# Seven block products for two tiles' keys and values, and queries in 512 columns, in a linear-attention and gated-network kernel

## The chip, the cores and the metric

The kernel runs on one core of a Trainium2 chip. The metric is device time in microseconds; the median of three runs of the kernel before is 583.31 us (582.87 to 583.67).

## The reference

All matrix products are fp32. With 2048 tokens of width D = 512, 32 heads of 16 and F = 1376:

```python
xn = layernorm(x)                                  # (2048, 512)
q, k, v = heads(xn @ wqkv)                         # 32 heads of 16
phi(t)  = concat(softmax(t @ w_phi), softmax(-(t @ w_phi)))   # per head, 32 wide
kv, z   = phi(k)^T v, sum_s phi(k)                 # state, over all tokens
s = (phi(q) kv / (phi(q) z + 1e-6)) @ wo
g = silu((relu(xn @ W_gate) * (xn @ W_up)) @ W_down)
out = x + s * g
```

The state needs all keys and values before the first query can be finished.

## The kernel before, in words

**Split products.** Each fp32 product is made of three fp32r matmuls: an operand is kept as a high part (rounded to fp32r by ScalarE) and a low part (the rest, subtracted on VectorE or GpSimd). `mm3` issues low x high, high x low, high x high for each 128 rows of the contraction. A "product" of 256 contraction rows is thus six matmuls.

**Token loop.** Tokens come in 16 tiles of 128, in the order of `order`: tiles of blocks 2 and 3 alternate, then those of blocks 0 and 1 (a block is 512 tokens). Tiles 2m and 2m + 1 make pair m: one tile of each block. Per tile n of the loop `for n in range(N)`: layernorm (sums on ScalarE in `norm_stats`, one power on GpSimd and two tiny operations on VectorE in `norm_scale` and `norm_apply`), transposition on TensorE with two copies on ScalarE (`turn`: `hi_xt`, `full_xt`) and the low part on VectorE (`lo_xt`); keys and values (`project`: 12 matmuls of 512 columns each); `features` (max, min, shift, exponentials, values' high and low parts, sums, reciprocal into PSUM, scaling); `features_split` (high part of phi on ScalarE, low part on GpSimd, and a DMA issued by GpSimd that adds phi to `zacc`); `query` for the tile before (24 matmuls of 256 columns, copied out and stored); `kv_products` of two tiles before (eight matmuls of 256 columns into four PSUM banks that stay until the end of the loop). The key weights are `wk` folded with w_phi on TensorE (`fold`), as are the query weights.

**Gated network.** `gate_up` computes gate and up of one 128-wide slice f (eleven slices) for a pair of blocks with seven products instead of eight (Strassen's scheme in Winograd's form): the transposed inputs `XT` hold blocks A11, A12, A22 and four sums S1 to S4 (`sums_x`, `sums_hi`, `sums_lo`), and `f_prep` makes the weights' differences and their parts (wa, wb, wc, wd) on GpSimd and ScalarE and stores them for the second half. The block A21, not wanted by the seven products, sits in a buffer of its own. Down products follow in chunks of two slices. Queries are finished (`q_pair`, `q_back`) beside this, and `out_tile` ends each half. There are two halves (blocks 0 and 1, then 2 and 3); the inputs of the second are stored and reloaded.

**Order of work.** Instructions of each engine run in the order written. Work in generators (weights' preparation, queries) is put in between by the object `pace`, which counts an estimated clock; constants such as `AHEAD`, `START` and the 20 in `pace.add(all_queries(0), 20)` set when it may begin. `AHEAD = (2, 3)` has slices 2 and 3 prepared in the token loop. `B8, B4, B2` are the numbers of 8, 4 and 2 KB buffers.

The lines of the scaling and the state of PSUM:

```python
        nc.vector.reciprocal(pv[:, 0:64], sm)
        phi = e if n else zacc
        nc.vector.tensor_tensor(groups(phi), groups(e), pv[:, 0:64].unsqueeze(2).to_broadcast([P, 64, DH]), op=ALU.mult)
        ...
            PKV.extend(ps((P, 2, 256), name=s) for s in ("pkv", "pkv", "pkv", "pseed"))
```

Of the kernel before, what the change touches and what calls it, by code (L numbers as in the profile page):

```python
# [13 lines left out]
P = 128  # L14
S = 2048
D = 512
# [12 lines left out]
B8, B4, B2 = 3, 10, 41  # L29
LEAD = 3  # L30
# [118 lines left out]
def layer_kernel(ctx: ExitStack, tc: tile.TileContext, x, wkT, wqT, wv, wo, wf, cst, out):  # L149
# [3 lines left out]
    pp = ctx.enter_context(tc.tile_pool(name="pp", bufs=8, space=bass.MemoryType.PSUM))  # L153
# [56 lines left out]
    N = len(order)  # L210
    X = {}
# [8 lines left out]
    def w_tile(name):  # L220
        return [(u2((P, D), f"{name}h", F32R), u2((P, D), f"{name}l", F32R)) for k in range(KD)]
# [8 lines left out]
    def rows(w):  # L230
        return lambda k: w[k]

    def fold(w, raw, k):

        p = ps(name="pfold")
        for j in range(KD):
            nc.tensor.matmul(p[:, j * P:(j + 1) * P], raw[:, j * P:(j + 1) * P], bd_sb[:, j, :],
                             start=True, stop=True)
        if w is WQ:
            return lambda: split(*w[k], p)  # L240
        return lambda: split(*map(by_parity, w[k]), even_first(p))


    XT = sb.tile([P, 7, 2, 2, BT], F32R, tag="XT", name="XT")
    pace.shared = XT.name
    A21, A21P, XN, XF, SF = {}, {}, {}, {}, {}

    def norm_stats(n):
        xt = X.pop(n)
        xn = u2((P, D), "xn")  # L250
        sm, ss, rs, bias = small(1, "lm"), small(1, "lv"), small(1, "lr"), small(1, "lb")
        nc.scalar.activation(xn, xt, AF.Copy, scale=-1.0 / D, accum_out=sm)
        nc.scalar.activation(xn, xt, AF.Square, bias=sm, accum_out=ss)
        XN[n] = xn, xt, bias, rs, sm, ss

    def norm_scale(n):
        xn, xt, bias, rs, sm, ss = XN[n]
        nc.vector.tensor_scalar(rs, ss, 1.0 / D, 1e-5, op0=ALU.mult, op1=ALU.add)
        nc.gpsimd.tensor_tensor(rs, rs, mhalf, op=ALU.pow)

    def norm_apply(n):
        xn, xt, bias, rs, sm, ss = XN[n]
        nc.vector.tensor_scalar(bias, sm, rs, None, op0=ALU.mult)
        nc.scalar.activation(xn, xt, AF.Identity, bias=bias, scale=rs)
        XN[n] = xn
# [16 lines left out]
    def cols(n):  # L282
        i = order[n][1]
        return slice(i * P, (i + 1) * P)
# [8 lines left out]
    def xt_parts(n, s):  # L293

        if n % 2 == 0:
            return [(XT[:, A11:A12 + 1, s, :, cols(n)], slice(0, 2))]
        if n not in A21:
            if n % 4 == 1:
                A21P[n // 4] = u4((P, 2, 2, 2 * P), "a21", F32R)
            c = n // 2 % 2 * P  # L300
            A21[n] = A21P[n // 4][:, :, :, c:c + P]
        return [(A21[n][:, s], 0), (XT[:, A22, s, :, cols(n)], 1)]

    def hi_xt(n, p):
        for to, c in xt_parts(n, 0):
            nc.scalar.activation(to, p[:, c], AF.Copy)
# [5 lines left out]
    def lo_xt(n, p):  # L312
        for (to, c), (hi, _) in zip(xt_parts(n, 1), xt_parts(n, 0)):
            add(nc.vector, to, p[:, c], f32(hi), ALU.subtract)

    def turn(m, full=True):
        p = transpose_x(m)
        hi_xt(m, p)
        if full:
            full_xt(m, p)  # L320
        return m, p

    def sums_x(n):

        x0, x1 = XF.pop(n - 1), XF.pop(n)
# [5 lines left out]
        SF[n] = sa, sb_  # L331

    def sums_hi(n):
        for s, c in zip(SF[n], (S1, S3)):
            nc.scalar.activation(XT[:, c:c + 2, 0, :, cols(n)], s, AF.Copy)

    def sums_lo(n):
        for s, c in zip(SF.pop(n), (S1, S3)):
            add(nc.gpsimd, XT[:, c:c + 2, 1, :, cols(n)], s, f32(XT[:, c:c + 2, 0, :, cols(n)]), ALU.subtract)

    def xt_cols(n):
        c = cols(n)
        if n % 2 == 0:
            return lambda k: (XT[:, k // 2, 0, k % 2, c], XT[:, k // 2, 1, k % 2, c])
        return lambda k: ((XT[:, A22, 0, k % 2, c], XT[:, A22, 1, k % 2, c]) if k // 2 else
                          (A21[n][:, 0, k % 2, :], A21[n][:, 1, k % 2, :]))

    xt_spill = dram((P, 7, 2, 2, BT), "xts")

    def spill_x(n):  # L350
        nc.sync.dma_start(xt_spill[:, :, :, :, cols(n)].rearrange("p c s k t -> p (c s k) t"),
                          f32(XT[:, :, :, :, cols(n)].rearrange("p c s k t -> p (c s k) t")))


    VH, PHI, PQ, EK = {}, {}, {}, {}
    PKV = []

    def project(n, w, name):
        p = ps(name=name)
        mm3(p, xt_cols(n), rows(w), range(KD))  # L360
        return p

    def query(n):

        b, h, j = order[n - n % 4 + n % 4 // 2][0], n // 4, n % 2
        c = slice(h % 2 * 2 * P, (h % 2 + 1) * 2 * P)

        def x_of(k):
            if n % 4 < 2:
                return XT[:, k // 2, 0, k % 2, c], XT[:, k // 2, 1, k % 2, c]  # L370
            if k // 2:
                return XT[:, A22, 0, k % 2, c], XT[:, A22, 1, k % 2, c]
            return A21P[h][:, 0, k, :], A21P[h][:, 1, k, :]
        p = ps((P, 2, 2 * P), name="pq")
        for d in range(2):
            w = slice((2 * j + d) * P, (2 * j + d + 1) * P)
            mm3(p[:, d, :], lambda k: [t[:, w] for t in WQ[k]], x_of, range(KD))
        if n % 4 == 3:
            A21P.pop(h)
        t = u2((P, 2, 2 * P), "pqs")  # L380
        nc.scalar.activation(t, p, AF.Copy)
        q = 2 * b + h % 2
        PQ[q, j] = dram((P, 2, 2 * P), f"pq{q}{j}")
        pace.when(t, lambda: nc.sync.dma_start(PQ[q, j], t))

    def features(n, pk, pv, between):

        vhl = u4((P, NG, 2, 64), "vhl", F32R)
        pvg = pv.rearrange("p (g f) -> p g f", g=NG)
        pkv_ = pk.rearrange("p (h f) -> p h f", f=DH)  # L390
        sm = small(64, "sm", 2)
        e = u4((P, H, 2, DH), "ek")
        mx = sb.tile([P, 2, H], F32, tag="mx", bufs=2, name="mx")
        nc.vector.tensor_reduce(mx[:, 0, :], pkv_, op=ALU.max, axis=AX.X)
        nc.vector.tensor_reduce(mx[:, 1, :], pkv_, op=ALU.min, axis=AX.X)
        for s in range(2):
            top = mx[:, s, :].unsqueeze(2).to_broadcast([P, H, DH])
            a, b = (top, pkv_) if s else (pkv_, top)
            nc.vector.tensor_tensor(e[:, :, s, :], a, b, op=ALU.subtract)
            nc.scalar.activation(e[:, :, s, :], e[:, :, s, :], AF.Exp)  # L400
            if s == 0:
                nc.scalar.activation(vhl[:, :, 0, :], pvg, AF.Copy)
        between()
        add(nc.vector, vhl[:, :, 1, :], pvg, f32(vhl[:, :, 0, :]), ALU.subtract)
        nc.vector.tensor_reduce(sm, groups(e), op=ALU.add, axis=AX.X)
        nc.vector.reciprocal(pv[:, 0:64], sm)
        VH[n] = vhl
        phi = e if n else zacc
        nc.vector.tensor_tensor(groups(phi), groups(e), pv[:, 0:64].unsqueeze(2).to_broadcast([P, 64, DH]), op=ALU.mult)
        EK[n] = phi  # L410

    def features_split(n):
        phi = EK.pop(n)
        phl = u8((P, NG, 2, P), "phl", F32R)
        split(phl[:, :, 0, :], phl[:, :, 1, :], flat(phi).rearrange("p (g f) -> p g f", g=NG), nc.gpsimd)
        if n:
            nc.gpsimd.dma_start(zacc, phi, accum_op=ALU.add)
        PHI[n] = phl

    def kv_products(n):  # L420
        phl, vhl = PHI.pop(n), VH.pop(n)
        if n == 0:
            PKV.extend(ps((P, 2, 256), name=s) for s in ("pkv", "pkv", "pkv", "pseed"))
# [7 lines left out]
    def two(name, apart):  # L431
        if apart:
            return [u2((P, 2, 2, P), name) for c in range(2)]
        t = u4((P, 2, 2, 2, P), name)
        return [t[:, c] for c in range(2)]
# [3 lines left out]
    def f_load(f):  # L439
        RAW[f] = two("rawg", f not in AHEAD), u2((P, D), "rawd")  # L440
        for c in range(2):
            nc.sync.dma_start(RAW[f][0][c].rearrange("p k s f -> p (k s f)"), wf[f][:, c * 512:(c + 1) * 512])
        nc.sync.dma_start(RAW[f][1], wf[f][:, 1024:])

    def w_pair(name):
        return u2((P, 2, 2, P), name, F32R), u2((P, 2, 2, P), name, F32R)
# [9 lines left out]
    def f_prep(f, keep=True):  # L456


        rg, rd = RAW.pop(f)
        b11, b12, b21, b22 = (rg[c][:, :, s, :] for c in range(2) for s in range(2))  # L460
        ta, tb = two("tab", keep)
        yield "gpsimd", b22
        add(nc.gpsimd, tb[:, 0], b12, b11, ALU.subtract)
        add(nc.gpsimd, ta[:, 1], b22, b12, ALU.subtract)
        wa = w_pair("wa")
        yield "scalar", b11
        for c in range(2):
            nc.scalar.activation(wa[0][:, c], rg[c][:, :, 0, :], AF.Copy)
        put(f, 0, wa[0])
# [4 lines left out]
        yield "scalar", ta  # L474
        nc.scalar.activation(wb[0], ta, AF.Copy)
        put(f, 2, wb[0])
        yield "gpsimd", wa[0]
        for c in range(2):
# [774 lines left out]
```

## Time and profile before

| | |
|---|---|
| median of three runs | 583.31 us |
| the profiled execution | 582.29 us |
| its span, first to last instruction | 580.3 us |
| TensorE busy | 567.5 us |
| GpSimd busy | 407.6 us |
| VectorE busy | 377.9 us |
| ScalarE busy | 297.9 us |
| granted TensorE clock | 1.0 |

In rows of the profile PE is TensorE's matmuls, PEld its weight loads, DVE VectorE, ACT ScalarE, POOL GpSimd. Nearly all rows have line 52, that of the helper through which all instructions are issued, so they are told apart by tile names. Rows of the timeline begin with the start, then the length, both in us; neighbouring instructions of an engine overlap a little, so the spacing of two starts is what one costs in a row of them.

### The profile page before, as it was taken

How to read it: one execution, taken by the hardware profiler on the slowest of the kernel's cores; microseconds unless marked ns; L12 is line 12 of the kernel's file. 1: busy time of each engine (PE TensorE's matmuls, PEld its weight loads, DVE VectorE, ACT ScalarE, POOL GpSimd, SP SyncE). 2: the span in 40 equal slices, each digit the busy share in tenths (PEclk: the TensorE clock that was granted, in tenths of full speed). 3: DMA queues.
4: the chain of work that ended last, by engine and by line, in shares of the span. 5: the costliest groups of instructions: out<-in, count | busy, mean ns of one | idle time of the engine just before them, and what ended most of it. 6: DMA issues, size and time to landing. Idle time of an engine off the chain costs nothing.

```text
span 580.3 us, 8580 instructions
## 1 busy us (share of the span) xinstructions
PE 567.5 (98%) x2848; PEld 478.5 (82%) x2848; DVE 377.9 (65%) x558; ACT 297.9 (51%) x536; POOL 407.6 (70%) x342
## 2 busy tenths in 40 slices
PE   8899999999999999999999999999999999999997
PEld 7788888889898788887888888787888888888786
DVE  3897766768564888998733332589698648943222
ACT  3796876766544547574543243234554634553500
POOL 0779888978868459999977514554568776976393
PEclk9999999999999999999999999999999999999999
DMA  8358899874499928797888999993566775459972
GB/s 299 104 159 222 231 288 291 237 207 99 138 251 283 370 78 274 241 307 255 276 279 281 261 384 406 380 389 127 150 213 201 221 227 188 117 171 311 291 216 108
DMA packets 82523, 138.25 MB, mean 238 GB/s; under 512 B 7600, under 2 KB 30512, under 8 KB 81584
## 3 DMA queue, kind: packets, MB, share of 16 engines
q1 hardware_dynamic: 79024, 125.60, 63.8%
q0 software_dynamic: 3312, 12.06, 11.0%
q8 instruction: 22, 0.36, 0.2%
q14 instruction: 21, 0.17, 0.1%
q10 hardware_dynamic: 144, 0.07, 0.0%
HBM read 77.14 MB, written 52.69 MB: 224 GB/s over the span
## 4 chain that ended last, share of the span: by engine, by line
PE 71%; POOL 9%; DMA 9%; issue 4%; DVE 3%; ACT 2%; SPq 0%; POOLq 0%; ACTq 0%; DVEq 0%
PE py L52 16%; PE pseed L52 12%; PE pd L52 8%; PE pa L52 8%; PE pso L52 8%; PE pq L52 5%; PE pv L52 4%; PE pk L52 4%; DMA wol<-wo 3%; PE pnum L52 2%; DMA pql<-pq 2%; POOL phl L52 2%; POOL XT L52 1%; DMA ws<-wd 1%; PE pkv L52 1%
## 5 line engine op out<-in xcount | busy, mean ns | idle before, releaser
L52 PE MATMUL py<-fdh,hl 128*128 128x512 f32 x176 | 68.8, 391 | 0.6 <-POOL hl L52 0.6
L52 PE MATMUL py<-fdh,hh 128*128 128x512 f32 x176 | 68.5, 389 | 0.0
L52 PE MATMUL py<-fdl,hh 128*128 128x512 f32 x176 | 68.5, 389 | 0.0
L52 POOL TENSOR_TENSOR hl<-e,hh 128x512 fp32r<-128x512 f32 x22 | 29.2, 1328 | 55.8 <-ACT hh L52 54.1
L52 PE MATMUL pa<-XT,wa 128*128 128x512 f32 x264 | 67.6, 391 | 0.0
L52 PE MATMUL pseed<-XT,wb 128*128 128x512 f32 x240 | 62.0, 393 | 1.4 <-ACT u L52 1.0
L52 PEld LDWEIGHTS pa<-XT,wa 128*128 128x128 f32 x264 | 49.2, 188 | 10.4 <-issue 0.5
L52 PEld LDWEIGHTS pseed<-XT,wb 128*128 128x128 f32 x240 | 44.4, 188 | 13.2 <-ACT u L52 3.3
L52 POOL TENSOR_TENSOR phl<-ek,phl 128x1024 fp32r<-128x1024 f32 x15 | 36.5, 2434 | 24.5 <-ACT phl L52 24.5
L52 DVE TENSOR_TENSOR y<-py,y 128x512 f32<-128x512 f32 x40 | 27.6, 691 | 39.9 <-PE py L52 39.7
L52 POOL TENSOR_TENSOR hl<-u,hh 128x512 fp32r<-128x512 f32 x22 | 29.4, 1335 | 19.0 <-ACT hh L52 17.3
L52 POOL TENSOR_TENSOR ez<-eq,zB 128x1024 f32<-128x1024 f32 x16 | 39.4, 2473 | 1.6 <-ACT eq L52 1.6
L52 PEld LDWEIGHTS py<-fdh,hl 128*128 128x128 f32 x176 | 33.0, 188 | 8.2 <-POOL hl L52 1.4
L52 PEld LDWEIGHTS py<-fdh,hh 128*128 128x128 f32 x176 | 33.0, 188 | 6.9
L52 PEld LDWEIGHTS py<-fdl,hh 128*128 128x128 f32 x176 | 33.1, 188 | 6.8
L52 POOL TENSOR_TENSOR y<-y,ys 128x512 f32<-128x512 f32 x24 | 31.1, 1297 | 9.0 <-ACT ys L52 9.0
L52 PE MATMUL pq<-XT,wqh 128*128 128x256 f32 x192 | 35.4, 282 | 0.0
L52 POOL TENSOR_TENSOR ol<-of,oh 128x1024 fp32r<-128x1024 f32 x8 | 19.4, 2439 | 22.2 <-DMA ol<-eq 11.7
L52 PE MATMUL pv<-wvh,XT 128*128 128x512 f32 x96 | 33.2, 400 | 1.0 <-ACT pqs L52 1.0
L52 PE MATMUL pd<-XT,wc 128*128 128x512 f32 x132 | 33.9, 390 | 0.0
L52 PE MATMUL pd<-XT,wd 128*128 128x512 f32 x132 | 33.6, 389 | 0.0
L52 DVE TENSOR_TENSOR e<-pd,e 128x512 f32<-128x512 f32 x22 | 15.1, 687 | 27.5 <-PE pd L52 19.6
(176 smaller groups left out, 1603.4 us busy)
## 6 DMA issues: line engine op xcount, KB each, us to landing
zacc<-ek POOLq DMA_DIRECT2D x15, 512.0 KB, 5.8
xts<-XT SPq DMA_DIRECT2D x4, 1792.0 KB
XT<-xts SPq DMA_DIRECT2D x7, 1024.0 KB, 14.9
wa<-ws SPq DMA_DIRECT2D x26, 256.0 KB, 3.0
wb<-ws SPq DMA_DIRECT2D x26, 256.0 KB, 5.2
wc<-ws SPq DMA_DIRECT2D x26, 256.0 KB, 4.2
rawg<-wf SPq DMA_DIRECT2D x22, 256.0 KB, 3.7
ws<-wa SPq DMA_DIRECT2D x22, 256.0 KB, 2.3
```

The costliest lines, as they stand in the source:

```text
L52: return self.tc.keep_in_program_order(op(*a, **k))
```

## The change

Pairs 2 to 7 take keys and values together in the seven-product scheme that the gated network has: the 512 x 1024 weight (keys beside values) is cut into blocks B11, B21 (keys) and B12, B22 (values) with differences T1 to T4, and the inputs' sums S1 to S4 are those of the network. Pairs 0 and 1 keep eight products, and the differences are made beside them. For pairs 0 and 1 the sums are made later, beside slices 8 and 9. Tile e = 2m, o = 2m + 1:

```diff
-A11, A12, A22, S1, S2, S3, S4 = range(7)
+A21, A22, A11, A12, S1, S2, S3, S4 = range(8)
-B8, B4, B2 = 3, 10, 41
+B8, B4, B2 = 2, 24, 14
-AHEAD = (2, 3)
-START = (12, 15)
+START = (14, 14)
-    pp = ctx.enter_context(tc.tile_pool(name="pp", bufs=8, space=bass.MemoryType.PSUM))
+    pp = ctx.enter_context(tc.tile_pool(name="pp", bufs=7, space=bass.MemoryType.PSUM))
+    seed = pp.tile([P, BT], F32, tag="seed", bufs=1, name="seed")
     def norm_scale(n):
-        nc.vector.tensor_scalar(rs, ss, 1.0 / D, 1e-5, op0=ALU.mult, op1=ALU.add)
+        nc.gpsimd.tensor_scalar(rs, ss, 1e-5, None, op0=ALU.add)
         nc.gpsimd.tensor_tensor(rs, rs, mhalf, op=ALU.pow)
+        nc.gpsimd.tensor_scalar(bias, sm, rs, D ** 0.5, op0=ALU.mult, op1=ALU.mult)
+    def key_scale(n):
+        e, pk, sm = EK[n]
+        r = sm if pk is None else pk[:, 0:64]
+        nc.vector.reciprocal(r, sm)
+        nc.vector.tensor_tensor(groups(e), groups(e), r.unsqueeze(2).to_broadcast([P, 64, DH]), op=ALU.mult)
+    def query(h, d, ks=range(KD)):
+        mm3(p, lambda k: [t[:, k % 2, w] for t in WQ[k // 2]],
+            lambda k: [XT[:, k // 2:k // 2 + 3:2, s, k % 2, c] for s in range(2)], ks, 0 in ks, KD - 1 in ks)
+    for m in range(2, M):
+        e, o = 2 * m, 2 * m + 1
+        pa = ps(name="pa")
+        product(pa, A11, "B11", m, True)
+        nc.scalar.activation(seed, pa, AF.Copy)
+        key_split(e - 2)()
+        query((m - 1) // 2, d + 1)
+        query_out((m - 1) // 2, d + 1)
+        product(seed, S2, "T2", m)
+        nc.scalar.activation(u, seed, AF.Copy)
+        collect = key_split(o - 2)
+        norm_stats(e + 4); norm_scale(e + 4)
+        product(pa, A12, "B21", m)
+        kv_products(e - 2)
+        key_shift(e, pa)
+        sums_x(m + 1)
+        product(seed, S3, "T3", m)
+        nc.scalar.activation(w, seed, AF.Copy)
+        norm_stats(o + 4); norm_scale(o + 4)
+        product(pd, S1, "T1", m, True)
+        key_exp(e)
+        norm_apply(e + 4); norm_apply(o + 4)
+        add(nc.vector, w, pd, w)
+        value_hi(o, w)
+        value_lo(o)
+        key_total(e)
+        product(seed, A22, "T4", m)
+        product(pd, S4, "B22", m)
+        add(nc.vector, u, pd, u)
+        mx = bounds(seed)
+        kv_products(o - 2)
+        collect()
+        px = turn(e + 4)
+        lo_xt(*px)
+        value_hi(e, u)
+        value_lo(e)
+        key_shift(o, seed, mx)
+        sums_hi(m + 1)
+        sums_lo(m + 1)
+        key_scale(e)
+        query(h, d)
+        query_out(h, d)
+        key_exp(o)
+        px = turn(o + 4)
+        key_total(o)
+        lo_xt(*px)
+        key_scale(o)
-            run(gate_up(f, used, rest))
+            run(gate_up(f, nc.gpsimd if half else nc.vector, used, rest))
-                    queries = pace.add(all_queries(0), 20)
+                    queries = pace.add(all_queries(0), 6)
```

(Two calls on a line and the missing conditions for the first and last pairs are shortenings of this text.) `value_lo` runs on GpSimd, `key_split` is the splitting of phi with its DMA returned as `collect`. Each pair has two queries, now of 12 matmuls of 512 columns. The last argument of `gate_up` shown is the engine of the low half hl of the network's hidden values: VectorE in the first half. The first slice is computed like the others, the separate `gate_up_apart` is gone; the last query, and the first half's last output tile, are issued behind the first product of a half's first slice. Small tiles are sized so that the larger buffers begin at multiples of 512 bytes. A21 is now part of XT, and the state's parts take its place after the loop.

More of the change, by code (lines that the diff above doesn't have):

```diff
@@ L728, in q_pair @@
         yield "vector", pv[1]
-        bounds(1)
-        shift(1)
+        bound(1)
+        shifted(1)
         if q + 1 < NP:
```

710 lines of the change are left out of this document (401 added, 309 removed).

## The prediction

> **What bounds the kernel now.** I read the page's busy times and chain of waits first, then three stretches in the windows view (the first four token tiles, the other twelve, the first half of the gated network), then who TensorE waited for.
>
> ```profile
> span 580.3 us, 8580 instructions
> ...
> PE 567.5 (98%) x2848; PEld 478.5 (82%) x2848; DVE 377.9 (65%) x558; ACT 297.9 (51%) x536; POOL 407.6 (70%) x342
> ...
> PE 71%; POOL 9%; DMA 9%; issue 4%; DVE 3%; ACT 2%; SPq 0%; POOLq 0%; ACTq 0%; DVEq 0%
> ```
> ```profile
> 0.00:54.00 54.00, 49.37 (x296) 44.17 (x297) 39.25 (x75) 38.41 (x78) 31.50 (x37) 1.00 0.62 193
> 54.00:176.00 122.00, 120.82 (x744) 107.37 (x743) 83.41 (x129) 77.77 (x148) 101.17 (x96) 1.00 0.80 220
> 176.00:338.00 162.00, 160.57 (x733) 131.57 (x732) 111.34 (x157) 81.06 (x157) 123.67 (x115) 1.00 0.80 266
> ```
> ```profile
> PE pxT L52 <- DVE lr L52: 2.0, 1, 2.0
> ...
> PE pv L52 <- ACT pqs L52: 1.0, 2, 0.7
> ```
>
> The window columns are PE, PEld, DVE, ACT, POOL. TensorE is the bound in every stage: 120.8 of 122 us in the token loop, and its longest wait anywhere is 2.0 us. The reader should also see that POOL is second in the loop (101 of 122). So a removed matmul is worth its spacing, as long as no other engine takes TensorE's place. The spacing comes from the chain (start, length, count):
>
> ```profile
> 54.25 2.75 PE pk L52 x12
> ...
> 130.69 2.84 PE pq L52 x24
> ...
> 134.47 2.75 PE pk L52 x12
> ...
> 176.05 1.39 PE pa L52 x6
> ...
> 337.93 16.32 PE py L52 x72
> ```
>
> A 512-column matmul takes 2.75/12 = 0.229 us in the projections and 16.32/72 = 0.227 in the down products; a 256-column one 2.84/24 = 0.118. Tile 4's keys start at 54.25, tile 12's at 134.47, the gated network at 176.05: four pairs of tiles take 80.2 us (20.06 each), and the last two pairs, with one more query and one more set of key-value products behind them, 41.6.
>
> **The change part by part.** *Seven products.* A pair has 42 instead of 48 projection matmuls: 6 x 0.229 = 1.37 us for six pairs, 8.2. *Queries.* 12 matmuls of 512 for 24 of 256: 2.84 - 12 x 0.227 = 0.12 us, sixteen times, 1.9. Together 10.1 us of TensorE, 1.61 in each pair of the loop. The Trainium skill ("TensorE: Matmul & The Clock Gate", Back-to-back issue gap) gives N/2.4 + 2.5 ns, so 109 and 216 ns; by it a query saves 0.03 us and all of them 0.5, and the forecast below would be up to 1.4 us higher. The trace's 118 and 227 differ from it, and the sum goes by them.
>
> *What the products add.* Each pair gets three more ScalarE copies (pa into seed, seed into u, seed into w) and two VectorE additions, the low halves of both values go from VectorE to GpSimd, and so do two small operations of each layernorm. PSUM for rotating tiles falls from four to three (seven buffers less the four of the key-value sums). Everything is issued in written order, so what counts is the longest loop through the queues. I find it like this. In pair m GpSimd's order is: low part of phi(e-2), collecting DMA, low part of phi(o-2), norm scale (e+4), four input sums, norm scale (o+4). ScalarE's normalisation of tile o+4 waits for the last of these. Behind it stand, in ScalarE's order: high half of value o, turn(e+4) (two copies), high half of value e, two high parts of the sums, query copy, two exponentials, turn(o+4) (two copies), the next pair's seed copy, the next phi high part; and GpSimd's next low part waits for that one. The prices are starts to starts in stretches without idle time, GpSimd first, then ScalarE:
>
> ```profile
> 62.43 2.43 POOL L52 TENSOR_TENSOR phl<-ek,phl 128x1024 fp32r<-128x1024 f32 x1 [2.79 <-ACT phl L52]
> 64.80 0.84 POOL L52 DMA_DIRECT2D zacc<-ek  x1
> 65.43 1.54 POOL L52 TENSOR_TENSOR XT<-sa,XT 128x512 fp32r<-128x512 f32 x1
> ...
> 67.95 0.77 POOL L52 TENSOR_TENSOR lr<-lr,mhalf 128x1 f32<-128x1 f32 x1
> 68.49 0.93 POOL L52 TENSOR_TENSOR sa<-xf 128x256 f32<-128x256 f32 x1
> 69.19 0.93 POOL L52 TENSOR_TENSOR sb<-xf 128x256 f32<-128x256 f32 x1
> 69.89 0.92 POOL L52 TENSOR_TENSOR sa<-sa,xf 128x256 f32<-128x256 f32 x1
> 70.89 0.74 POOL L52 TENSOR_TENSOR sb<-xf,sa 128x256 f32<-128x256 f32 x1
> 71.59 2.43 POOL L52 TENSOR_TENSOR phl<-ek,phl 128x1024 fp32r<-128x1024 f32 x1
> ```
> ```profile
> 60.26 0.61 ACT L52 ACTIVATE XT<-sa 128x512 fp32r<-128x512 f32 x1
> 60.78 0.62 ACT L52 ACTIVATE XT<-sb 128x512 fp32r<-128x512 f32 x1
> 61.30 1.05 ACT L52 ACTIVATE phl<-ek 128x1024 fp32r<-128x1024 f32 x1
> 62.25 0.80 ACT L52 ACTIVATE xn<-xt,lb,lr 128x512 f32<-128x512 f32 x1
> ...
> 63.97 0.63 ACT L52 ACTIVATE ek<-ek 128x512 f32<-128x512 f32 x1
> 64.49 0.60 ACT L52 ACTIVATE vhl<-pv 128x512 fp32r<-128x512 f32 x1
> 64.96 0.64 ACT L52 ACTIVATE ek<-ek 128x512 f32<-128x512 f32 x1
> ...
> 69.78 0.80 ACT L52 ACTIVATE xn<-xt,lb,lr 128x512 f32<-128x512 f32 x1
> 70.49 0.57 ACT L52 ACTIVATE XT<-pxT 128x512 fp32r<-128x512 f32 x1
> 70.97 0.58 ACT L52 ACTIVATE xf<-pxT 128x512 f32<-128x512 f32 x1
> ```
>
> GpSimd: two low parts at 2.37 (62.43 to 64.80), the DMA 0.63, the four sums 3.10 (68.49 to 71.59): 8.47, and two norm scales. ScalarE: normalise 0.71 (69.78 to 70.49), four copies out of PSUM or of values, queries and seed at 0.47 (64.49 to 64.96), four turn copies at 0.48, four operations at 0.52 (60.26 to 60.78, 63.97 to 64.49), phi 0.95 (61.30 to 62.25): 0.71 + 1.88 + 1.92 + 2.08 + 0.95 = 7.54. The hand-overs between the two engines I put at 0.4 (phi ends at 62.35 on ScalarE and GpSimd starts at 62.43; the rest is the part of a last instruction that the spacing leaves out).
>
> A norm scale is now three dependent GpSimd operations on 128x1, of which only the power was there. Rows near the other two:
>
> ```profile
> L1245 POOL MEMSET const-float32-0.0<- 128x1 f32 x1 | 0.1, 99 | 0.2 <-issue 0.2
> ```
> ```profile
> L52 POOL TENSOR_TENSOR lr<-lr,mhalf x12: 549/798/849, 25.2 to 128.3; 128x1 f32<-128x1 f32 x12
> ...
> L52 DVE TENSOR_SCALAR lb<-lm,lr x12: 206/212/216, 25.8 to 129.1; 128x1 f32<-128x1 f32 x12
> ```
>
> Bounds for one norm scale: 0.54 + 0.1 with the rest hidden, or three times the power's 0.54 and twice the 0.3 us that the third sum lost on its predecessor (1.00 instead of 0.70 to the next start), 2.2. I take 0.9, the power plus two at about VectorE's 0.15 to 0.21, the nearest operation of that kind. The loop is then 8.47 + 1.8 + 7.54 + 0.4 = 18.2 us.
>
> One thing more sits in it: the scaling of keys now reads its reciprocals from SBUF instead of PSUM, so this 1024-element VectorE operation has both inputs in SBUF. Such an operation is there today only as pTl:
>
> ```profile
> 254.29 2.13 DVE L52 TENSOR_TENSOR pTl<-ez,pTh 128x1024 fp32r<-128x1024 f32 x1
> ```
> ```profile
> 255.28 2.28 POOL L52 TENSOR_TENSOR wb<-tab,wb 128x512 fp32r<-128x512 f32 x1
> ```
> ```profile
> L52 DVE TENSOR_TENSOR pTl<-ez,pTh x6: 1215/1240/2129, 220.1 to 287.8; 128x1024 fp32r<-128x1024 f32 x6
> ```
> ```profile
> L52 POOL TENSOR_TENSOR wb<-tab,wb 128x512 fp32r<-128x512 f32 x11 | 17.0, 1542 | 0.0
> ...
> L52 POOL TENSOR_TENSOR tab<-rawg 128x256 f32<-128x256 f32 x22 | 17.8, 878 | 0.9 <-PE py L52 0.9
> ```
>
> The two overlapped, and GpSimd's took 2.28 where its mean is 1.54; bounds 0 and about 1 us for each of the two scalings in a pair. Scaling o comes when GpSimd works on the next low part, inside the loop; scaling e during the low parts of the sums, outside it. I count one: 19.2 us. That is above TensorE's own 20.06 - 1.61 = 18.45, so in these four pairs ScalarE and GpSimd set the pace: 4 x 19.2 = 76.8 instead of 80.2, -3.4. Of VectorE's additions none is on this loop; their cover is its 38 us idle in 122. The last two pairs have no layernorm and no turning, the loop is open there, and TensorE's gain counts in full: 2 x 1.61, -3.2.
>
> *The first four tiles* keep eight products. GpSimd gets four weight differences (4 x 2.37) and the low parts of T1 and T4 (4 x 1.54), about 15.6 us more, and loses two sets of sums; ScalarE gets twelve copies at about 0.5; VectorE four low parts and the statistics of two tiles. All still fit in 54 us by the windows row (39, 38 and 31 busy), but VectorE closely. Bounds: -2 (the 2.0 us wait for lr goes) and +6 (15.6 less GpSimd's idle before it is wanted, and VectorE late). I take +0.5. The loop starts with keys 2 and 3 not yet scaled and one pair of exponentials (1.04) ahead of the first phi: +1.0.
>
> *Weights of the gated network.* f = 2 and 3 are no longer prepared in the loop and f = 0, 1 only in its last pair, with the low parts on VectorE. One f costs GpSimd at most 4 x 0.88 and five low parts of 1.54, 11.2 us. f = 2 is wanted about 20 us into the network; bounds 0 and +5, taken +1.0. The low halves hl of half 0 move to VectorE, 22 operations with both inputs in SBUF; their cover is its 51 and GpSimd's 38 idle us of 162, price 0, if it fails a few us. The seeded first product, the last query and the last output tile put between f = 0's products, the sums fetched at f = 8 and 9, and buffers starting at multiples of 512 bytes: 0, hidden under TensorE; bounds -1 and +1.
>
> Sum: -3.4 - 3.2 + 0.5 + 1.0 + 1.0 = -4.1 us. The profiled execution took 582.29 (span 580.3 and 2.0 around it), so 578.2; the median of the runs is 1.0 above it, 583.31, so 579.2.
>
> **The rivals.** *TensorE keeps the pace.* The small GpSimd operations are nearly free and no scaling collides: 8.47 + 1.28 + 7.54 + 0.4 = 17.7, under 18.45. Then the whole 10.1 is won, and the first stage costs nothing: 573. For it: ScalarE and GpSimd have idle time in the loop today. Against: that idle time is waiting for each other (2.79 us before the low part at 62.43).
>
> *The loop through GpSimd is longer than before: slower.* Norm scale at 1.44 (0.54, two of 0.15 and two gaps of 0.3) and both scalings colliding: 8.47 + 2.88 + 7.54 + 0.4 + 2.0 = 21.3, 4 x 21.3 - 80.2 = +5.0; with -3.2 and +2.5 the time is 587.6. It decides from 20.2 us a pair, 1.0 above my number. For it speaks the row at 254.29; against, that it is the longest of six such operations. The Trainium skill ("SBUF — State Buffer", Who interferes with whom) states that a VectorE instruction with two SBUF inputs and a GpSimd instruction that reads SBUF exclude each other. The 2.28 us row agrees.
>
> *The first stage turns VectorE-bound* and ends 5 us later (its 39.25 us there grow by four low parts of 0.6, half a pTl, and two tiles' statistics to about 45, an estimate, and it starts only when the first tile has landed): 583.3, no change.
>
> **How the numbers follow.** Forecast 0.40, TensorE keeps the pace 0.22, longer loop 0.26, late first stage 0.12. A measurement here tells 0.2% (1.2 us) from nothing. Faster: 0.62. The late first stage mostly ends within 1.2 us: same 0.10, and its rest to slower: 0.28. The range is 571 (TensorE's full gain and its present waits) to 588 (the longer loop); the forecast alone is 576 to 582.
>
> **What would show it.** Right: pairs of about 19 us in the first four of the loop and 17 in the last two; TensorE waiting for ScalarE ahead of the seed products (T2) and ScalarE waiting for GpSimd ahead of xn; queries of 12 matmuls in 2.72 us. Wrong: pairs of 18 us without waits (573), or GpSimd rows of phl well over 2.43 and pairs above 20.2 (slower); a loop that starts well after 55 us; a wait at f = 2 for wa or wb.

## The result and the profile after

The changed kernel takes 607.22 us (median of four runs, 604.49 to 610.54) beside 583.49 (582.87 to 583.81) for the kernel before: a ratio of 1.041 (95% interval 1.036 to 1.046). The profiled execution took 607.11. The first lines of its page:

```profile
span 605.3 us, 8090 instructions
...
PE 565.1 (93%) x2616; PEld 462.3 (76%) x2616; DVE 428.7 (71%) x536; ACT 310.1 (51%) x557; POOL 407.7 (67%) x339
```

VectorE has 51 us more than before, GpSimd as much as before. The windows view, cut at the loop's first product, at pair 6, at the network and at its second half (columns PE, PEld, DVE, ACT, POOL, clock, DMA share, GB/s):

```profile
0.00:61.00 61.00, 51.04 (x260) 41.43 (x261) 44.58 (x69) 35.49 (x67) 33.90 (x34) 0.97 0.51 170
61.00:150.00 89.00, 76.16 (x363) 61.32 (x361) 67.40 (x68) 59.35 (x115) 65.86 (x73) 0.98 0.44 119
150.00:187.60 37.60, 34.60 (x164) 28.33 (x165) 34.78 (x32) 20.82 (x36) 29.57 (x25) 1.00 0.58 152
187.60:393.60 206.00, 197.27 (x885) 160.52 (x884) 148.57 (x198) 102.35 (x190) 137.13 (x118) 0.99 0.89 299
393.60:605.00 211.40, 206.01 (x951) 170.75 (x949) 133.35 (x172) 92.04 (x152) 141.24 (x91) 1.00 0.70 224
```

In the pairs no engine is full: TensorE is busy 76 of 89 us, VectorE 67, GpSimd 66. That is a loop of waits, not a full engine. The first starts on TensorE in the trace mark the stages (us; e1, e5 and e11 are experiments below):

| | before | after | e1 | e5 | e11 |
|---|---|---|---|---|---|
| start to the loop's first product | 54.3 | 61.1 | 59.5 | 59.0 | 61.1 |
| pairs 2 to 5 | 80.2 | 88.8 | 81.4 | 73.8 | 73.9 |
| pairs 6 and 7 | 41.6 | 37.8 | 40.3 | 40.3 | 35.9 |
| half 0 | 195.0 | 205.9 | 202.9 | 201.5 | 203.7 |
| half 1 to the span's end | 209.3 | 211.7 | 211.7 | 211.7 | 211.6 |
| span | 580.3 | 605.3 | 595.8 | 586.3 | 586.2 |
| gaps on TensorE, summed | 19 | 55 | 45 | 36 | 36 |

The last row is worked out from the trace: each distance between two starts, less the number of matmuls times their spacing (0.227, 0.119 and 0.111 us for 512, 256 and 128 columns). Matmul records that are missing count as gaps, a few us in each column, and so does what a lower clock takes: the granted clock is 0.992 on the mean after the change and 1.0 before, 0.8% of 605 us, about 5 us. So the change takes about 10 us of matmuls away, as forecast, and adds some 35 us of gaps. The last query moved from the pairs into half 0 and the last output tile from half 0 into half 1, 12 matmuls or 2.7 us each; a set of eight key-value products (1.0 us) moved from the pairs into half 0 too.

Who waits for whom, TensorE first, then ScalarE (us in total, times, longest):

```profile
PE pkv L51 <- POOL phl L51: 8.8, 5, 2.0
PE seed L51 <- ACT u L51: 8.5, 10, 2.2
PE seed L51 <- ACT seed L51: 4.1, 4, 2.0
PE pa L51 <- DVE XT L51: 3.7, 4, 1.5
```
```profile
ACT phl L51 <- DVE ek L51: 27.6, 14, 3.1
...
ACT xn L51 <- POOL lb L51: 13.2, 6, 2.8
```

The scaling of keys in the groups view, before and after (behind the bar the busy us of all, the mean ns of one, and the idle us before them):

```profile
L52 DVE TENSOR_TENSOR ek<-ek,pv 128x1024 f32<-128x1024 f32 x15 | 18.3, 1220 | 0.5
```
```profile
L51 DVE TENSOR_TENSOR ek<-ek,sm 128x1024 f32<-128x1024 f32 x15 | 41.7, 2777 | 0.5
```

One cycle of a pair in the timeline of the changed kernel, TensorE, VectorE, GpSimd:

```profile
105.38 0.50 PE L51 MATMUL pa<-B11h,XT 128*128 128x512 f32 x1 [1.47 <-DVE XT L51]
...
127.65 0.50 PE L51 MATMUL pa<-B11h,XT 128*128 128x512 f32 x1 [1.42 <-DVE XT L51]
```
```profile
104.63 0.69 DVE L51 TENSOR_TENSOR XT<-pxT,XT 128x512 fp32r<-128x512 f32 x1 [2.84 <-ACT xf L51]
...
106.94 3.84 DVE L51 TENSOR_TENSOR ek<-ek,sm 128x1024 f32<-128x1024 f32 x1
...
113.00 2.44 DVE L51 TENSOR_TENSOR ek<-ek,sm 128x1024 f32<-128x1024 f32 x1
...
126.90 0.69 DVE L51 TENSOR_TENSOR XT<-pxT,XT 128x512 fp32r<-128x512 f32 x1 [2.81 <-ACT xf L51]
```
```profile
106.86 1.58 POOL L51 TENSOR_TENSOR XT<-sa,XT 128x512 fp32r<-128x512 f32 x1
108.13 1.56 POOL L51 TENSOR_TENSOR XT<-sb,XT 128x512 fp32r<-128x512 f32 x1
...
116.69 2.38 POOL L51 TENSOR_TENSOR phl<-ek,phl 128x1024 fp32r<-128x1024 f32 x1 [1.52 <-ACT phl L51]
119.05 0.23 POOL L51 TENSOR_SCALAR lr<-lv 128x1 f32<-128x1 f32 x1
...
124.27 0.26 POOL L51 TENSOR_SCALAR lb<-lm,lr 128x1 f32<-128x1 f32 x1
```

Read it as a ring. VectorE goes from the low part of tile e+4 (104.63) through the shift, two reciprocals, the scaling of e, the sums of o, the low part of o+4, to the end of the scaling of o (115.44): 10.8 us. ScalarE's high part of phi follows (to 116.69, 1.2), then GpSimd's low part, norm scale, sums and second norm scale (to 124.53, 7.8), then ScalarE's normalise of o+4 and its copies, and VectorE's low part of the next tile e+4 begins at 126.90 (2.4). Together 22.3 us, the pair. The scaling of e starts at 106.94 with GpSimd's low parts of the sums and ends 1.1 us after them (110.78 against 109.69): VectorE's instruction stood until GpSimd's were done. So did the scaling of o: it ends at 115.44, again 1.1 us after GpSimd's low part (112.01 to 114.36 in the same view), and 1.2 us is what a scaling takes undisturbed.

### The profile page after: what moved, and what is told of

Same layout as the page of the kernel before. It is cut to its first block, busy times and chain, and to the rows that moved or that the text cites. A ratio compares the mean times of both kernels' runs of the same rounds, so it can differ in the third digit from the quotient of the medians.

```text
span 605.3 us, 8090 instructions
## 1 busy us (share of the span) xinstructions
PE 565.1 (93%) x2616; PEld 462.3 (76%) x2616; DVE 428.7 (71%) x536; ACT 310.1 (51%) x557; POOL 407.7 (67%) x339
## 3 DMA queue, kind: packets, MB, share of 16 engines
q1 hardware_dynamic: 78304, 122.97, 59.3%
q0 software_dynamic: 3312, 12.06, 10.2%
## 5 line engine op out<-in xcount | busy, mean ns | idle before, releaser
L51 PE MATMUL py<-fd,hh 128*128 128x512 f32 x528 | 130.7, 389 | 0.0
L51 PEld LDWEIGHTS py<-fd,hh 128*128 128x128 f32 x528 | 99.0, 188 | 21.0 <-DVE hh L51 0.4
L51 PE MATMUL seed<-XT,wb 128*128 128x512 f32 x264 | 70.6, 401 | 10.6 <-ACT u L51 6.4
L51 PEld LDWEIGHTS seed<-XT,wb 128*128 128x128 f32 x264 | 48.5, 190 | 26.5 <-ACT u L51 10.7
L51 PEld LDWEIGHTS pa<-XT,wa 128*128 128x128 f32 x264 | 49.3, 188 | 10.2
L51 POOL TENSOR_TENSOR phl<-ek,phl 128x1024 fp32r<-128x1024 f32 x15 | 35.9, 2392 | 27.5 <-ACT phl L51 27.5
L51 DVE TENSOR_TENSOR e<-pd,e 128x512 f32<-128x512 f32 x22 | 15.0, 684 | 41.6 <-PE pd L51 29.8
L51 DVE TENSOR_TENSOR ek<-ek,sm 128x1024 f32<-128x1024 f32 x15 | 41.7, 2777 | 0.5
L51 PE MATMUL pso<-wo,oh 128*128 128x512 f32 (+1 forms) x136 | 39.8, 376 | 0.0
L51 ACT ACTIVATE seed<-pa 128x512 f32<-128x512 f32 x28 | 16.5, 589 | 40.4 <-PE pa L51 32.5
L51 ACT ACTIVATE hh<-u 128x512 fp32r<-128x512 f32 x22 | 13.9, 632 | 44.7 <-DVE u L51 42.6
L51 PE MATMUL seed<-XT,wc 128*128 128x512 f32 x132 | 33.7, 390 | 0.0
L51 DVE TENSOR_TENSOR u<-pd,u 128x512 f32<-128x512 f32 x34 | 23.2, 683 | 13.2 <-PE pd L51 8.4
L51 PEld LDWEIGHTS pso<-wo,oh 128*128 128x128 f32 x136 | 25.0, 188 | 4.8
```

Source lines behind the costliest of these rows:

```text
L51: return self.tc.keep_in_program_order(op(*a, **k))
```

## The experiments

All times stand beside runs of the kernel before on the same chip.

**e1: only the reciprocals, from SBUF to PSUM tiles that are no longer used.** *Theory*: the slowed scaling makes the loop of waits long. *Rival*: the loop is long without it.

```diff
-    def key_scale(n):
-        r = sm if pk is None else pk[:, 0:64]
+    def key_scale(n, r):
+        r = flat(r)[:, 0:64]
...
-        key_scale(e)
+        key_scale(e, px[1] if e + 4 < N else rs_[0])
```

(`rs_` holds pa and pd of the pair; `flat(r)` stands for the flattening of a PSUM tile. Tiles 0 to 3 use pk, pv and px.)

> The changed kernel with one thing undone: the reciprocals of the keys' sums go to PSUM again (into tiles whose contents are used up), so the scaling of a key tile has one input in SBUF. Port theory (a VectorE operation with both inputs in SBUF waits for GpSimd): its mean falls from 2777 ns to about 1220, the first four pairs of the loop from 22.3 us to 19 to 20, the last two from 18.9 to about 17.5, the first stage ends 1 to 3 us earlier, the waits at the start of the network shrink by about 3: 588 to 593 us in all. Order theory (the loop GpSimd norm scale, normalise, ScalarE, phi sets the pair by itself and the scaling only fills time that is waited out anyway): pairs stay at 21.5 or more, 602 us or more.

Measured 596.74 us, ratio 1.022 (1.017 to 1.027), between the two expectations: 10 us of the 24 are this. The scaling and the waits of the pairs in e1:

```profile
L51 DVE TENSOR_TENSOR ek<-ek,pxT 128x1024 f32<-128x1024 f32 x9 | 11.0, 1221 | 0.3
```
```profile
PE pa L51 <- ACT pqs L51: 8.0, 6, 1.7
```
```profile
76.28 0.26 POOL L51 TENSOR_SCALAR lb<-lm,lr 128x1 f32<-128x1 f32 x1
...
96.28 0.26 POOL L51 TENSOR_SCALAR lb<-lm,lr 128x1 f32<-128x1 f32 x1
```

```profile
80.33 0.59 ACT L51 ACTIVATE pqs<-pq 128x512 f32<-128x512 f32 x1
```
```profile
80.97 0.50 PE L51 MATMUL pa<-B11h,XT 128*128 128x512 f32 x1 [1.65 <-ACT pqs L51]
```
```profile
88.65 2.39 POOL L51 TENSOR_TENSOR phl<-ek,phl 128x1024 fp32r<-128x1024 f32 x1 [0.97 <-ACT phl L51]
```

Pairs 3 to 5 take 20.0 us each, not TensorE's 18.4: behind the ring through VectorE stood a second one. From lb (76.54) ScalarE normalises and makes seven more copies, the last of them pqs (to 80.92, 4.4 us); that frees one of the three rotating PSUM banks, and only then pa starts; TensorE needs 6.0 us to the end of the T2 product, ScalarE 1.6 for u and phi's high part, GpSimd 7.9 for its low part, both norm scales and the four sums (88.65 to 96.54). Together 20.0. The first stage did not end earlier, as the theory had it: the loop starts at 59.5, and at 58.8 and 58.5 in e3 and e8, which keep the slowed scaling.

**e2: the kernel before, with only the reciprocals moved into SBUF.**

```diff
-        nc.vector.reciprocal(pv[:, 0:64], sm)
+        nc.vector.reciprocal(sm, sm)
```

> The kernel before with that one thing done: reciprocals in SBUF instead of PSUM, nothing else. Port theory: the scaling (1220 ns) takes 2 us or more in the mean and the kernel is slower, by less than in the changed kernel because its token loop has more slack: 585 to 592 us. Order theory: within 1.5 us of before.

Measured 593.71 us, ratio 1.017 (1.013 to 1.021), a little more than the theory had. The one operand costs 10 us in a kernel that has nothing else of the change:

```profile
L52 DVE TENSOR_TENSOR ek<-ek,sm 128x1024 f32<-128x1024 f32 x15 | 47.8, 3187 | 0.5
```
```profile
PE pk L52 <- DVE ek L52: 6.8, 7, 1.5
```

The Trainium skill ("SBUF — State Buffer", Who interferes with whom) calls the port that VectorE shares with GpSimd an exclusive lock. By that the trace agrees, on the side that I had not priced: the instruction with both inputs in SBUF takes 2.78 to 3.19 us on the mean, with one input in PSUM 1.22, beside the same GpSimd work.

**e3 and e4: the low halves hl of half 0 on GpSimd,** in the changed kernel (e3) and in e1 (e4).

```diff
-            run(gate_up(f, nc.gpsimd if half else nc.vector, used, rest))
+            run(gate_up(f, nc.gpsimd, used, rest))
```

> The changed kernel with the low halves of the hidden values in the first half back on GpSimd, alone. Port theory: the 22 operations (943 and 851 ns on VectorE in place of about 690) are part of the late ScalarE copies between products; 1 to 4 us faster than the changed kernel, 603 to 606. Rival (GpSimd is the scarce engine there, 29 us more on it make the weights late): no change or slower, 607 to 612.

> Both of these undone in the changed kernel. If the two act in different stages their gains add: 585 to 591 us. If the first half's waits come only from keys that are late, the second adds nothing to the first.

Measured 623.5 us (ratio 1.069, 1.065 to 1.073) and 614.31 (1.051, 1.047 to 1.056): 16 to 18 us slower, more than any expectation had. This piece of the change is right where it is: GpSimd is busy without a gap at the end of half 0 in e3 (13.9 of the 14 us from 330 to 344), and the queries' features come late:

```profile
PE pnum L51 <- ACT pTh L51: 11.2, 2, 9.6
```

The granted clock is 0.50 for 17 us in both runs, from within that wait on (last section). Matmuls of 256 columns then come every 0.21 us and those of 512 every 0.43, which costs another 3 us by estimate.

**e5 and e8: the order on GpSimd,** the second norm scale ahead of the sums, in e1 (e5) and in the changed kernel alone (e8).

```diff
-        if m + 1 < M:
-            sums_x(m + 1)
         product(seed, S3, "T3", m)
...
             norm_scale(o + 4)
+        if m + 1 < M:
+            sums_x(m + 1)
```

> The changed kernel with the reciprocals in PSUM (as in e1), and the second norm scale of a pair (for tile o+4) issued on GpSimd ahead of the four sums instead of behind them. Theory A, the cycle: in e1 each pair took 20.0 us because GpSimd's lb for tile o+4 (96.5 us) is followed by ScalarE's normalise, five more copies and the query's copy, then the next pair's first product, the copy u, phi's high part, phi's low part, two norm scales and the four sums, and so back to lb. The sums are 2.9 us of it (92.37 to 95.30). Without them the cycle is 17.1 us, under TensorE's own 18.3 us; the gaps before pa (1.65 us in each pair) go, pairs take about 18.4 us, and the time falls by 1.6 x 5 = 8 us to about 589. Rival, the banks: the gap before pa is a wait for one of three rotating PSUM banks that ScalarE empties late because of its own amount of work; then pairs stay at 20.0 us and the time stays at 596 to 597.

> The changed kernel with only the order of e5: the second norm scale ahead of the four sums, reciprocals where the change put them. Theory A, the cycle as I predicted it, with the collision inside: the changed kernel's pairs of 22.3 us contain the same 2.8 us wait of ScalarE for lb, and the sums go out of the chain: pairs of about 19.6 to 20 us, 4 to 5 pairs, so 9 to 12 us less, 595 to 598. Rival, the slowed scaling alone sets the pairs: the wait turns up at another place (phi's high part on VectorE's ek, 27.6 us over 14 times already), pairs stay above 21.5 us, and the time is 604 to 607.

e5: 588.99 us, ratio 1.013 (1.009 to 1.016); pairs of 18.4 us, as the ring theory had it, and the waits for pqs ahead of pa fall from 8.0 to 2.4 us. e8: 600.75, ratio 1.032 (1.029 to 1.035), between its two expectations: pairs of 20.8 us on the mean. The sums left the ring, but now the scalings meet more of GpSimd's work (mean 3.09 us), and the wait stands before the key-value products:

```profile
PE pkv L51 <- POOL phl L51: 9.4, 5, 2.3
```

So each edit opens one ring, and only both bring TensorE's pace. In e5 another instruction of the collided kind is left, the low part of a weight in pair 6, and TensorE waits for what stands behind it:

```profile
156.94 5.44 DVE L51 TENSOR_TENSOR wa<-rawg,wa 128x512 fp32r<-128x512 f32 x1 [2.06 <-ACT wa L51]
```
```profile
157.06 1.72 POOL L51 TENSOR_TENSOR tab<-rawg 128x256 f32<-128x256 f32 x2
158.46 2.67 POOL L51 TENSOR_TENSOR phl<-ek,phl 128x1024 fp32r<-128x1024 f32 x1
160.81 2.17 POOL L51 TENSOR_TENSOR tab<-rawg,tab 128x256 f32<-128x256 f32 x2
```
```profile
PE pd L51 <- DVE u L51: 2.5, 1, 2.5
```

Behind that wait the granted clock is 0.50 for 3.4 us (from 166.5), another 1.7 us.

**e6 and e7: start of the queries, and T2, T3 on GpSimd,** each on top of e5.

```diff
-                    queries = pace.add(all_queries(0), 6)
+                    queries = pace.add(all_queries(0), 20)
```
```diff
-    difference_parts("T2", t2, nc.vector)
+    difference_parts("T2", t2, nc.gpsimd)
```

(and T3 likewise.)

> As e5, and the queries' features of half 0 (with the state before them) start after 20 rows of TensorE time instead of 6, as in the kernel before. Theory A, the place does not matter: the state's copies on ScalarE (eight of kvt, eight of zB, 4.4 us together) and VectorE's share stand in front of the network's copies wherever they start; the stalls of some 4 us near 204 to 216 us move and stay, and the time is that of e5 within 1 us. Rival, the crowd: the stalls come from the state and the first queries falling together with the weights of f = 1 and 2; started later they fall beside TensorE's work, and the time is 3 to 5 us below e5.

> As e5, and the low parts of T2 and T3 in the first stage are taken by GpSimd instead of VectorE. Theory A, VectorE's queue sets the end of the first stage: it is relieved of 3.49 + 1.29 us of work at 41 to 46 us, the waits of TensorE on VectorE's ek and XT (0.5 and 1.5 us) go, and the loop starts at about 57.5 instead of 59.5 us: 2 us below e5. Rival, the chain over GpSimd sets it: GpSimd gets about 5.1 us more work in front of phi(1), the norm scale of tile 6 and the sums; ScalarE's normalise of tiles 6 and 7 waits longer for lb, the loop starts at 62 to 64 us, and the time is 3 to 5 us above e5.

e6: 588.5 us, ratio 1.009 (1.005 to 1.013), the same as e5: whether the queries begin after 6 or after 20 rows does not matter. e7: 590.67, ratio 1.014 (1.011 to 1.018). The loop starts at 62.0 instead of 59.0, as the rival had it, but then pair 6 has no collision (the network starts at 171.8 instead of 173.1), half 0 takes 3.2 us longer, and the time rises by 1.7 only.

**e9 and e10: weights' low parts on GpSimd, and the order of the first stage.** e9 is e5 with the first line; e10 adds the second block.

```diff
-        lo, low = ("vector", nc.vector) if f < 2 else ("gpsimd", nc.gpsimd)
+        lo, low = "gpsimd", nc.gpsimd
```
```diff
     query(0, 2)
-    difference_parts("T2", t2, nc.vector)
     key_split(1)()
...
     norm_scale(6)
-    difference_parts("T3", t3, nc.vector)
     pk = project(2, "pk", "B11", "B21")
...
     key_shift(2, pk)
+    difference_parts("T2", t2, nc.vector)
...
-    norm_apply(7)
     px = turn(6)
     lo_xt(*px)
+    norm_apply(7)
+    difference_parts("T3", t3, nc.vector)
...
-    key_total(2)
...
     key_shift(3, pk)
+    key_total(2)
```

> As e5 (reciprocals in PSUM, second norm scale ahead of the sums), and the low parts of the weights of f = 0 and 1 are taken by GpSimd, as the kernel before does, instead of VectorE. Theory A, a second collision of the same kind: in e5 VectorE's low part of wa, with both sources in SBUF, took 5.44 us at 156.94 while GpSimd took differences and a low part, the maxima of the pair's keys queued behind it, and TensorE waited 2.55 us for VectorE's u at 162.5; later the lows of f = 1 (187.5 to 190.8) stood before the state's kvt, ScalarE waited 2.97 us for it, and TensorE 1.99 us for ScalarE's u. Both go: 4 to 6 us less than e5, 583 to 585. Rival, GpSimd becomes short: it gets 2 x 5.9 us more work at the head of the network, pa waits for weights at f = 0 or 1, and the time is within 1 us of e5 or above it.

> As e9, and in the first stage four pieces change place in the queues: T2's parts and T3's parts behind the shift of tile 2's keys, the normalise of tile 7 behind the copies of tile 6, the sums of keys 2 behind the shift of tile 3's keys. Theory A, the order of VectorE's and ScalarE's queues sets the end of the first stage: TensorE's waits at 47 to 59 us in e5 (0.51 on ek, 1.43 on XT, 2.61 on ek) lose 2 to 3 us, the loop starts at about 56.5 instead of 59 us, and the time is 2 to 3 us under e9, 580 to 582. Rival, the stage is bound by the amount of work that change added there: T2 and T3 come late, TensorE waits for them in the loop's first pair instead, and the time is that of e9 within 1 us.

e9: 599.69 us, ratio 1.026 (1.022 to 1.031): the rival, and more. The 2.5 us in pair 6 are gone, but at f = 1 the weights come late:

```profile
PE pa L51 <- POOL wa L51: 4.6, 1, 4.6
```

e10: 596.57, ratio 1.024 (1.020 to 1.027). It is 3 us under e9, and its loop starts 1.5 us earlier. But e9 was 2.8 us later already at its first transposition (11.70 us against 8.92: its first weights landed 1.2 us later, and the clock was at half behind them), and the intervals overlap: that the order of the first stage gains anything is not shown.

**e11 to e14: the pieces together.** e11 is e10 with f = 1 back on VectorE (`if f == 1`); e12 issues the last collecting DMA behind the last key-value products; e13 puts `yield 24,` ahead of the products pz; e14 moves T2's parts behind tile 6's copies and T3's behind `value_lo(2)`.

> As e10, but only the weights of f = 0 have their low parts on GpSimd; those of f = 1 go back to VectorE. Theory A, e9 joined two things: at f = 0 the collision in the last pair is gone (TensorE's wait of 2.55 us for u at 162.5 in e5 is not in e9), at f = 1 GpSimd's longer queue made TensorE wait 4.64 us for wa. Each at its better place: e5 less 2.7 us for f = 0 and less 2 to 3 us for the first stage, so 583 to 585, level with the kernel before. Rival, the lows of f = 0 on GpSimd delay everything GpSimd does at the head of the network, whoever takes f = 1: the network starts as late as in e10, and the time is 591 to 597.

> As e11, and GpSimd's accumulating transfer of the last tile's features is issued behind the last key-value products instead of directly behind the low part of phi. Theory A: in e5 GpSimd stood 3.5 us on that transfer (178.4 to 185.2, for the one before on the same sums), the differences of f = 1 stood behind it, then VectorE's lows, the state's kvt, ScalarE's copies, and TensorE's waits of 2.0 and 1.35 us near 195 to 207; issued later, the differences come 3 to 4 us earlier and 2 to 3 us of these waits go: 2 to 3 us below e11. Rival: the transfer's end then sets the sums' products (pz) and ScalarE's zB copies, and the wait only changes its name: e11 within 1 us.

> As e12, and the products of the features' sums (pz) and what follows them come 24 rows of planned TensorE time (some 5 us) later. Theory A, the wait of 4.83 us that TensorE had in e12 before pz, for the accumulating transfer, was only a matter of order: the transfer ends beside products of the network, at most 1 us of the wait is left, and the time is 3 to 5 us below e12, 582 to 584. Rival, crowding: ScalarE's zB copies come 5 us later in front of the copies u and seed of the network, the first queries come later too, and the wait turns up before seed; the time is that of e12 within 1 us.

> As e13, and in the first stage T2's parts come behind tile 6's copies and T3's behind the low parts of tile 2's values. Theory A, order: TensorE's two waits there (2.2 us before pxT of tile 7, 1.1 to 1.6 us before pv of tile 3) lose 2 to 3 us together, and the time is 2 to 3 us below e13. Rival, work: VectorE and ScalarE have the same pieces to do before the loop's first products, T2 and T3 are late for them, and the time is that of e13 within 1 us.

587.61 (ratio 1.009, 1.008 to 1.011), 586.68 (1.009, 1.006 to 1.011), 588.34 (1.009, 1.007 to 1.011) and 590.02 us (1.011, 1.009 to 1.014). e11 ends between its two theories, and in e12 the rival held. e13 and e14 gained nothing either, as their rivals had it, but each ended 1.7 us above the run that it starts from, where the rivals allowed 1 us. In pairs 6 and 7 e11 gets what it should (35.9 us instead of 40.3), but its loop starts 2.1 us later than e5's, and half 0 is 2.2 us longer. The waits at its head only change their names, in e11, e12 and e13:

```profile
PE pz L51 <- DVE u L51: 3.6, 1, 3.6
```
```profile
PE pz L51 <- DMA zacc<-ek: 4.8, 1, 4.8
```
```profile
PE seed L51 <- ACT u L51: 4.5, 8, 1.4
PE seed L51 <- ACT seed L51: 3.2, 3, 1.5
```

**e15 and e16: work left out of half 0** (both from e11).

```diff
+        if f in (2, 3):
+            for i, t in enumerate([*wa, *wb, *wc, wd, *fd]):
+                nc.sync.dma_start(f32(flat3(t)), wspill[1][i])
```
```diff
-        sums_x(m)
-        for s, c in zip(SF.pop(m), (S1, S3)):
+        for n, c in zip((2 * m, 2 * m + 1), (S1, S3)):
+            t = XF.pop(n)
```

> As e11, but the preparation of the weights' slices 2 and 3 is left out: their tiles are filled by transfers with the parts of slice 1, so the output is not the reference's. GpSimd is spared 2 x 4 differences and 2 x 5 low parts (about 2 x 10 us at 0.78 and 1.28 us each), ScalarE 2 x 5 copies. Theory A, the preparation that the change moved from the token loop into half 0 makes it long: the stalls between 195 and 260 us go and half 0 falls from 203.7 us (e11) to 195 to 199, the time from 587.6 to 580 to 583. Rival: half 0 is paced by something else (the queries' features beside it, ScalarE's queue behind the state); half 0 stays at 202 to 205 us and the time at 586 to 589.

> As e11, but the sums of the first two pairs beside slices 8 and 9 are left out: what is stored for half 1 is the fetched inputs themselves, so the output is not the reference's. GpSimd is spared 2 x (4 x 0.74 + 2 x 1.28), 11 us, ScalarE four copies. Theory A, it is this work in half 0 that costs: its last 60 us shorten, half 0 falls by 2 to 4 us and the time to 584 to 586. Rival: GpSimd has time for it there, and nothing changes beyond 1 us.

587.66 us (ratio 1.009, 1.006 to 1.012) and 588.59 (1.010, 1.006 to 1.013), half 0 of 204.2 and 203.1 us: in both the rival held. What the change moved into half 0 does not make it long. In e5, e11, e13 and e15 half 1 begins at 374.3 to 375.0 us, whether half 0 began at 173.1, 171.0, 170.4 or 170.1; the other variants of e5 and e11 lie between 373.5 and 377.6, apart from e9 and e10 with their late weights (389.8 and 382.3). In e5 and e11 most of its gaps lie in the first 35 us (6.5 of 10.0 us and 8.6 of 12.1, worked out as in the table), around the state's products, where VectorE's and ScalarE's queues hold the state, f = 1 and the hidden values at once. A lead of the pairs is lost there: GpSimd stands for the transfer before on the same sums until it can issue the last one, in e5 and then in e11:

```profile
185.17 0.88 POOL L51 DMA_DIRECT2D zacc<-ek  x1 [3.52 <-DMA zacc<-ek]
```
```profile
184.23 0.87 POOL L51 DMA_DIRECT2D zacc<-ek  x1 [4.47 <-DMA zacc<-ek]
```

Half 0 begins 2.1 us earlier in e11, this issue 0.9, and ScalarE's u, for which TensorE then waits 2.0 us, begins at 198.2 in one and 198.3 in the other. But e13, where that issue stands behind the last key-value products and pz comes later, has only 3.0 us of gaps in the first 35 and 10.2 behind them, and its half 1 begins no earlier. Which piece is decisive stays open.

## Why the prediction was wrong, by its steps

*Held.* The spacings and the 10 us of matmuls; that waiting and not an engine's fullness would set the pairs; ScalarE's wait for lb ahead of xn, which I named as the sign; the seed waits; hl on VectorE (e3 and e4 say that it belongs there). Whether the seeded first product, the last query and the output tile cost nothing, as I had it, no run tells. The other-side rival asked for pairs above 20.2 us; they took 22.2, though on another path than it gave.

*The step that failed* is "Of VectorE's additions none is on this loop; their cover is its 38 us idle in 122", with "bounds 0 and about 1 us for each of the two scalings" and "I count one: 19.2 us". I gave the collision to GpSimd, the engine of the 2.28 us row. The row of pTl beside it stood at 2.13 us against 1.215 for its fastest, so VectorE's own loss was on the page. In the trace the two scalings of a pair take 3.84 and 2.44 us instead of 1.22 each, 3.8 us more, and both lie on the ring, that of e too, which I had put outside: 22.3 us a pair, instead of 19.2. e1 and e2 show it from both sides, 10 us each.

*The loop that I did find* was too short as well. Without the collision e1 takes 20.0 us a pair where 18.2 was forecast. The norm scale is 1.23 to 1.33 us from start to start (0.9 taken, 0.64 to 2.2 the bounds), and the ring does not run through ScalarE's turn(o+4) to phi(e), but through the PSUM bank that pqs frees and through 24 matmuls to phi(o). I had written that the rotating banks fall from four to three and put no price on it. e5 shows that without the sums in the ring the pairs reach 18.4, TensorE's own pace: the -3.4 us forecast for four pairs was +8.6 in the changed kernel and -6.4 in e5.

*Pairs 6 and 7*: -3.8 for -3.2, but 2.7 of it is the query moved out and 1.0 the key-value products; the gain of TensorE itself was lost to waits. In e1 and e5, where a low part of a weight collides, they take 40.3; that one I had put on VectorE without a price. In e11, where it does not, they take 35.9, 5.7 less than before, so 2.0 of the 3.2 came true there.

*First stage and loop start*: +6.9 for +1.5. Within the bounds of -2 to +6 plus 1.0, wrong in the choice. About 2.4 of it is spread between executions: e3 and e8 have the same first stage, and their loops start at 58.8 and 58.5, 4.5 and 4.3 later than before. In the profile of the changed kernel the first weights landed at 8.2 us, 0.8 and 1.0 later than in those two, and the clock stood at 0.50 for 3.4 us behind them. The rest is near the 5 us of the rival "The first stage turns VectorE-bound", beside a longer ring and not instead of it; VectorE is busy 44.6 us there, about the 45 that it named. That VectorE sets it is not shown: e7 takes two low parts from it and starts the loop at 62.0, and e5, e10 and e14, at 59.0, 60.8 and 59.3, start it no earlier than e3 and e8.

*Half 0*: +1.0 for the weights, 0 for the rest; measured +10.9. The last query, 8 key-value products (1.0) and the output tile that left explain about 1.0. The preparation of f = 2 and 3 (e15) and the sums (e16) cost nothing that shows. With the scalings' collisions and the ring gone it is still +6.5 in e5, mostly at the state's place. The prediction had no term for the state there, and the cause of these us stays open.

## What to carry to other kernels

Count where an instruction's operands lie before counting its elements: a VectorE operation with both inputs in SBUF beside a busy GpSimd lost 1.6 to 2.0 us on the mean here, and 10 us of the whole when it stood in a ring of waits, while a dead PSUM tile as the place of a 64-element operand cost nothing that shows. When engines have idle time and still nothing is full, write down all rings between them, PSUM banks among them, with the instruction of each engine that closes the ring; opening the longest gives only the distance to the second (e8: 6.5 us, e1: 10.5, both: 18.2). An instruction that nobody waits for soon (the sums) belongs behind the one that closes the ring.

## What the runs showed of the hardware that I had not expected

A collided instruction is not just slower: here it stood through a whole row of the other engine's instructions, those that started after it too. The 512-element low part at 156.94 in e5 took 5.44 us (the same form 1.15 elsewhere in that run, and 0.68 undisturbed: fd at 169.32). GpSimd's five operations from 157.06 overlap in the trace, except the last two, with a gap from 161.83 to 161.90; VectorE's ended at 162.38, 0.55 us behind the start of that gap.

TensorE's granted clock dropped after some short gaps. In the changed kernel, two stretches behind gaps of 1.9 and 2.2 us (windows view, the column behind POOL is the clock):

```profile
138.50:141.50 3.00, 3.00 (x8) 2.35 (x8) 1.62 (x2) 2.94 (x9) 2.56 (x2) 0.50 0.66 131
...
199.00:203.50 4.50, 4.34 (x16) 3.83 (x17) 0.00 (x0) 0.27 (x2) 3.67 (x4) 0.62 0.99 247
```

Matmuls of 512 columns then come every 0.42 us. Each such stretch costs about 1.6 us beside the gap itself. It does not follow every gap: three pairs ahead of the first had waits of the same size and kept the full clock, and what decides is not shown. The Trainium skill ("TensorE: Matmul & The Clock Gate", HAM oscillation) names gaps above some 3.4 us as the danger; the trace differs, gaps of about 2 us came ahead of both stretches.

Around e3's wait of 9.6 us (349.7 to 359.3) the clock stayed low for five times as long (in e4 from 343.4 to 360.4):

```profile
354.10:371.10 17.00, 8.75 (x26) 7.00 (x27) 7.59 (x8) 5.50 (x8) 1.51 (x3) 0.50 0.23 56
```

How often this happens differs between executions of one kernel, and the time goes with it: the five of e9 took 594.99, 598.18, 599.69, 600.72 and 603.24 us at granted clocks of 0.993, 0.989, 0.986, 0.983 and 0.980. Whether the clock or a wait ahead of it makes the difference is not shown.
